# Top-k attention and a mixer block on one core: q and k transposed by the vector engine from 32 x 32 blocks, and one way of masking for all batches

## The chip, the cores and the metric

The kernel runs on one core of one Trainium2 chip. A core has five engines with queues of their own: TensorE (PE in the profile, with its weight loads as PEld), VectorE (DVE), ScalarE (ACT), GpSimd (POOL) and SyncE (SP), which here only issues transfers. All data are float32. The metric is the device time of one execution in microseconds (us), the median of several runs.

## The reference

Eight batches, eight heads, 576 positions, 64 features a head. Attention keeps, in each row of scores, those that are at least the 32nd largest; the rest get weight 0. The result, with the heads side by side (512 channels), goes through a mixer: a low-rank product along the sequence (rank 32) that is added to its input, and two dense layers of 2048 hidden channels with a ReLU.

```python
def _attn_ref(q, k, v):                       # (8, 8, 576, 64) each
    scores = 1 / sqrt(64) * np.matmul(q, k.transpose(0, 1, 3, 2))
    kth = np.partition(scores, -32, axis=-1)[..., -32:-31]
    scores = np.where(scores >= kth, scores, -1e9)
    attn = np.exp(scores - np.max(scores, axis=-1, keepdims=True))
    attn = attn / (np.sum(attn, axis=-1, keepdims=True) + 1e-9)
    return np.matmul(attn, v)

def _moe_ref(x, U, V, w_ch1, w_ch2):          # x: (8, 576, 512)
    h = x.transpose(0, 2, 1) @ U @ V
    u = x + h.transpose(0, 2, 1)
    return u + np.maximum(u @ w_ch1, 0.0) @ w_ch2
```

## The kernel before

The kernel works on pairs of heads, g = 0 to 31, four to a batch (NPAIR = 4). The 576 positions of a pair are five rows of tiles, t = 0 to 4: four of 128 positions, in which each head is a chunk of 128 x 576 scores, and a last one of 64 positions, in which both heads lie in one chunk (64 partitions each). So a pair has nine chunks. A step n of the main loop is one row: g, t = divmod(n, 5). The instructions of PE, ACT, DVE and POOL stand in the order in which the program makes them; the order of SyncE's transfers is left to a scheduler.

Loading and transposing. q and k come with positions on the partitions; TensorE transposes them, four tiles of 128 x 128 to a PSUM buffer, and ScalarE copies them to SBUF, so that features lie on partitions in qkT. Each pair has three such pieces: q, k, and the ends of both (the last 64 positions).

```python
    def load(g):
        b, h0 = g // NPAIR, 2 * (g % NPAIR)
        ends = loads.tile([P, 2, D], F32, tag="ld_ends", name="ld_ends")      # pool loads: bufs=1
        for name, src in (("q", q), ("k", k)):
            t = loads.tile([P, NT, 2, D], F32, tag=f"ld_{name}", name=f"ld_{name}")
            for i in range(2):
                # one transfer a head, on SyncE's queue (two of the first pair on ScalarE's)
                queue.dma_start(t[:, :, i, :], src[b, h0 + i, 0:MAIN, :].rearrange("(p t) d -> p t d", t=NT))
        # ... two transfers for the ends, five for v (into va, vd, vt, three buffers of each)

    def prep(g):
        # ...
        for i in (0, 2, 1) if g == 0 else (0, 1, 2):
            if i == 2:
                tp = ps_t.tile([P, 2, TAIL], F32, tag="tp", name="tp")        # ps_t: two PSUM buffers
                nc.tensor.transpose(tp.rearrange("p i n -> p (i n)"), ends.rearrange("p h d -> p (h d)"), ident)
                nc.scalar.copy(qkT[:, :, MAIN:S], tp)
                yield
                continue
            tp = ps_t.tile([P, NT, P], F32, tag="tp", name="tp")
            for c in range(NT):
                nc.tensor.transpose(tp[:, c, :], tiles[i][:, c].rearrange("p h d -> p (h d)"), ident)   # L272
            copy = nc.vector.tensor_copy if g == 0 and i else nc.scalar.copy
            copy(qkT[:, i, 0:MAIN], tp.rearrange("p t n -> p (t n)"))                                   # L274
            yield
```

The top 32 of a chunk. VectorE finds eight maxima at a time (L352, L366) and takes them out of a copy (L362), four and three times. The eighth of the last maxima is the row's threshold. After that there are three ways to the weights E, by chunk:

- early: ScalarE takes the exponential of all scores ahead, and VectorE then sets those below the threshold to 0 and sums the rest (L372).
- pooled: GpSimd compares and adds a huge negative number to the scores below the threshold (L369, L370), and ScalarE takes the exponential and the sum afterwards (L318).
- gaps: ScalarE makes relu((threshold - score) x 2^96) (L386, L387), GpSimd subtracts that (L388), and ScalarE takes the exponential and the sum (L318).

```python
    def ways(g, t):                               # chunks that are (early, pooled, gaps)
        if g < 2 * NPAIR and (g, t) != (NPAIR - 1, NT):
            if (g, t) == (NPAIR - 1, NT - 1):
                return (0,), (), (1,)
            return (), (1,) if t < NT else (), (0,)
        return (0,), (1,) if t < NT else (), ()

    def eased(g, t):
        return bool(ways(g, t)[2])

    def front(g, t):                              # a generator; the main loop takes it piece by piece
        # ... maxima and match_replace, four pieces
        for c in pooled:
            nc.gpsimd.tensor_scalar(Es[c], chunks[c], ms[c][:, 7:8], NEG, ALU.is_lt, ALU.mult)
            nc.gpsimd.tensor_tensor(chunks[c], chunks[c], Es[c], ALU.add)
        for c in early:
            nc.vector.scalar_tensor_tensor(out=Es[c], in0=chunks[c], scalar=ms[c][:, 7:8], in1=Es[c],
                                           op0=ALU.is_ge, op1=ALU.mult, accum_out=sums[c])
        # ...
        yield
        for c in gaps:
            least = small.tile([P, 1], F32, tag="least", name="least", bufs=3)
            nc.scalar.mul(least, ms[c][:, 7:8], WIDEN)
            nc.scalar.activation(Es[c], chunks[c], AF.Relu, bias=least, scale=-WIDEN)
            nc.gpsimd.tensor_tensor(chunks[c], chunks[c], Es[c], ALU.subtract)
            yield
        for c in order:
            if c not in early:
                weigh(chunks[c], Es[c], nmax[:, c : c + 1], sums[c])          # L318, the exponential
        # ...
```

After that TensorE transposes E (turns: L408 twice, four tiles each, then L413 once, with copies L409 and L414 on ScalarE), multiplies by v (values: L442, L445, and L432 for the last row), and after the fifth row of a pair turns the result and makes the low-rank product (mixed: L466, L477, L489, L491). Scores of the next row are L300 (L287 for the last row), copied to SBUF by ScalarE (L311 to L313, L294).

The mixer's dense layers of one batch (mlp: L514 and L533, 128 x 256 or 128 x 320 a matmul; L561 turns the result back) are laid between the steps of a later batch by `fill()`, so much a step, at 0.91 of the full share up to step 42. The main loop from the second batch on:

```python
        ease = eased(*divmod(n - 1, CH))          # here = front of row n, last = front of row n - 1
        # ... (the first batch and the turn to the second)
        if ease:
            next(last, None)
        fill()
        next(turning, None)
        fill()
        next(turning, None)
        if eased(*divmod(n - 2, CH)):
            next(turning, None)
        fill()
        next(ready, None)                         # ready = prep(g + 1), made at t == 1
        fill()
        if ease:
            next(last, None)
        if n - 2 >= ALONE:
            values(*divmod(n - 2, CH))
        if n + 1 < STEPS:
            scores(*divmod(n + 1, CH))
        next(here, None)
        next_params(1)
        # ...
        fill()
        next(here, None)
        fill()
        if n <= STEPS:
            turning = turns(*divmod(n - 1, CH))
        if not ease:
            next(turning, None)
        fill()
        next(here, None)
        next(last, None)
        # ...
        next(here, None)
        fill()
```

Of the kernel before, what the change touches and what calls it, by code (L numbers as in the profile page):

```python
# [8 lines left out]
F32 = mybir.dt.float32  # L9
# [17 lines left out]
def kernel(  # L27
# [28 lines left out]
    nc = tc.nc  # L56
    B, H, S, D = q.shape
    P = 128
# [4 lines left out]
    NT, TAIL = 4, 64  # L63
    MAIN = NT * P
    HALF = S // 2
    assert S == MAIN + TAIL and D == 64 and H % 2 == 0 and C == 512 and TOPK % 8 == 0
    NPAIR = H // 2
    NP = B * NPAIR
    SCALE = 1.0 / float(D) ** 0.5
    NV = 3  # L70
    HT = 10
    PE, ACT = mybir.EngineType.PE, mybir.EngineType.Activation
    DVE, POOL = mybir.EngineType.DVE, mybir.EngineType.Pool
# [2 lines left out]
    loads = ctx.enter_context(tc.tile_pool(name="loads", bufs=1))  # L76
# [18 lines left out]

    vas = [const.tile([P, 2, NT, D], F32, name=f"va{i}") for i in range(NV)]
    vds = [const.tile([P, P], F32, name=f"vd{i}") for i in range(NV)]
    vts = [const.tile([P, 2, D], F32, name=f"vt{i}") for i in range(NV)]

    xs = [const.tile([P, NT + 1, P], F32, name=f"x{i}") for i in range(2)]  # L100
    for i in range(NV):
        nc.gpsimd.memset(vds[i], 0.0)
# [25 lines left out]
    def half(h):  # L128
        return slice(h * D, (h + 1) * D)
# [97 lines left out]
    raw, qkTs, S2s, uTs, XTs, dens = {}, {}, {}, {}, {}, {}  # L227
    probs, PTs = {}, {}

    def load(g):  # L230
        b, h0 = g // NPAIR, 2 * (g % NPAIR)
        tiles = []
        ends = loads.tile([P, 2, D], F32, tag="ld_ends", name="ld_ends")
        for name, src in (("q", q), ("k", k)):
            t = loads.tile([P, NT, 2, D], F32, tag=f"ld_{name}", name=f"ld_{name}")
            for i in range(2):
                queue = nc.scalar if g == 0 and i else nc.sync
                queue.dma_start(
                    t[:, :, i, :],
                    src[b, h0 + i, 0:MAIN, :].rearrange("(p t) d -> p t d", t=NT),  # L240
                )
            tiles.append(t)
        for i, src in enumerate((q, k)):
            nc.sync.dma_start(
                ends[half(i)], src[b, h0 : h0 + 2, MAIN:S, :].rearrange("h p d -> p h d")
            )
        va, vd, vt = (a[g % NV] for a in (vas, vds, vts))
        for i in range(2):
            nc.sync.dma_start(
                va[:, i], v[b, h0 + i, 0:MAIN, :].rearrange("(p t) d -> p t d", t=NT)  # L250
            )
            nc.sync.dma_start(vd[half(i), half(i)], v[b, h0 + i, MAIN:S, :])
        nc.sync.dma_start(vt[TAIL:P], v[b, h0 : h0 + 2, MAIN:S, :].rearrange("h p d -> p h d"))
        raw[g] = tiles, ends

    def prep(g):

        tiles, ends = raw.pop(g)
        qkT = attn.tile([P, 2, S], F32, tag="qkT", name="qkT")
        qkTs[g] = qkT  # L260
        for i in (0, 2, 1) if g == 0 else (0, 1, 2):
            if i == 2:
                tp = ps_t.tile([P, 2, TAIL], F32, tag="tp", name="tp")
                nc.tensor.transpose(
                    tp.rearrange("p i n -> p (i n)"), ends.rearrange("p h d -> p (h d)"), ident
# [10 lines that stand above are left out]
# [44 lines left out]
    def ways(g, t):  # L320

        if g < 2 * NPAIR and (g, t) != (NPAIR - 1, NT):
            if (g, t) == (NPAIR - 1, NT - 1):
                return (0,), (), (1,)
            return (), (1,) if t < NT else (), (0,)
        return (0,), (1,) if t < NT else (), ()

    def eased(g, t):  # L330
        return bool(ways(g, t)[2])

    def front(g, t):
# [16 lines left out]
        for c in order:  # L350
            ms[c] = first[:, c]
            nc.vector.max(ms[c], curs[c])  # L352
        yield
        early, pooled, gaps = ways(g, t)
        for i in range(1, TOPK // 8):
            if i == 1:
# [60 lines left out]
    def inverse(g, lo, hi):  # L417
        den = dens[g][:, lo:hi]
        if g == NPAIR - 1:
            nc.vector.tensor_scalar_add(den, den, 1e-9)  # L420
        nc.vector.reciprocal(den, den)

    def values(g, t):

        PT = PTs.pop((g, t))
        va, vd, vt = (a[g % NV] for a in (vas, vds, vts))
        O = ps_t.tile([P, P], F32, tag="tp", name="O")
# [76 lines left out]
    def mlp(b):  # L504
# [3 lines left out]
        for chunks, (lo, hi) in zip(PARTS, SPAN):  # L508
            w = hi - lo
            hTs = []  # L510
            for f in range(NF):
# [11 lines left out]
                if f % 2 == 0:  # L523
                    hT = mlpp.tile([P, 2, WIDE], F32, tag="hT", name="hT", bufs=HT)
                    hTs += [hT[:, 0], hT[:, 1]]
# [53 lines left out]
    CH = NT + 1  # L579
# [30 lines left out]
    t = 0  # L610
    for _ in prep(0):
        pass
    scores(0, 0)
    turning = ready = iter(())
    fronts = {}
    for n in range(STEPS + 2):
        g, t = divmod(n, CH)
        if n < STEPS:
            if t == 0 and g + 1 < NP:
                load(g + 1)  # L620
            if t == 1 and g + 1 < NP:
                ready = prep(g + 1)
            fronts[n] = front(g, t)
            next(fronts[n])
        here, last = fronts.get(n, iter(())), fronts.pop(n - 1, iter(()))
        if n >= ALONE - 1 and n <= ALONE:

            if n < ALONE:
                next(last)
                values(*divmod(n - 3, CH))  # L630
                list(turning)
                next(here)
                next(last)
                scores(*divmod(n + 1, CH))
                values(*divmod(n - 2, CH))
            list(turns(*divmod(n - 1, CH)))
            values(*divmod(n - 1, CH))
            if n < ALONE:
                next(here)
                next(here)  # L640
                inverse(g, 0, 2 * NT)
                mixing.append(mixed(g, 1))
                fill()
                next(here)
# [3 lines that stand above are left out]
            next(here)  # L648
            while mixing:
# [4 lines that stand above are left out]
            next(here)  # L654
            fill()
            next(here)
            next(here)
            fill()
            continue
        ease = eased(*divmod(n - 1, CH))  # L660
        if n < ALONE:
# [3 lines that stand above are left out]
            if n >= 3:  # L665
                values(*divmod(n - 3, CH))
                if (n - 3) % CH == NT:
                    mixing.append(mixed((n - 3) // CH, 3))
            list(turning)
            fill()  # L670
            next(here)
            if t < NT:
                next_params(1)
            fill()
            next(ready, None)
            next(here)
            next(last, None)
            fill()
            next(here)
            if t in (0, 1):  # L680
                next_params(1)
            next(here)
            fill()
            if n >= 1:
# [5 lines that stand above are left out]
        next(turning, None)  # L690
        fill()
        next(turning, None)
        if eased(*divmod(n - 2, CH)):
            next(turning, None)
        fill()
        next(ready, None)
        fill()
        if ease:
            next(last, None)
# [6 lines that stand above are left out]
        if n - 2 >= ALONE and (n - 2) % CH == NT:  # L706
            mixing.append(mixed((n - 2) // CH, 5))
        fill()
        next(here, None)
        fill()  # L710
        if n <= STEPS:
            turning = turns(*divmod(n - 1, CH))
        if not ease:
            next(turning, None)
        fill()
        next(here, None)
        next(last, None)
        if t in (1, 3):
            next_params(1)
        next(here, None)  # L720
        fill()
# [33 lines left out]
```

## Time and profile before

| | before |
|---|---|
| time, median of 3 runs | 1842.92 us (1842.66 to 1843.83) |
| span of the profiled execution | 1841.4 us |
| mean granted TensorE clock | 0.974 |
| PE busy | 1739.0 us, 94% |
| PEld busy | 1319.0 us, 72% |
| DVE busy | 1561.2 us, 85% |
| ACT busy | 1020.7 us, 55% |
| POOL busy | 682.3 us, 37% |
| transfers | 58.20 MB in 127294 packets |

The profile is of one execution. A group of instructions is named by line of the kernel, engine, operation and tiles, output before input: "L272 PE MATMUL tp<-ident,ld_q" is a matmul of line 272 that writes tile tp from tiles ident and ld_q. "<-" after an idle time names what ended it. The chain of waits is followed back from the last instruction: at each step to what released it, or to the instruction ahead of it on its engine. In a timeline of engines the time of a matmul holds its latency, so that successive matmuls overlap; in the chain they are laid end to end. A line of one of the stretches of time gives the busy us of each engine in it.

### The profile page before, as it was taken

The page shows a single profiled execution, that of the slowest core. Times are in us where ns is not written, and L with a number is a line of the kernel's source. Part 1 is how long each engine was busy: PE and PEld are TensorE (multiplying, and loading weights), DVE is VectorE, ACT ScalarE, POOL GpSimd, SP SyncE. Part 2 cuts the span into 40 slices and gives each one's busy share as a digit, 9 for nine tenths or more (in the row PEclk, how much of TensorE's full clock was granted, in tenths as well). Part 3 has the DMA queues.
Part 4 walks back from the last instruction along what each step waited for, and adds up shares of the span by engine and source line. Part 5 has one row for each costly group of instructions (what it writes and reads, how often), then busy time and mean ns, then how long its engine had stood idle before and what let it go on. Part 6 is the DMA issues. An engine that isn't in the chain of part 4 may idle for free.

```text
span 1841.4 us, 29144 instructions
## 1 busy us (share of the span) xinstructions
PE 1739.0 (94%) x10528; PEld 1319.0 (72%) x10528; DVE 1561.2 (85%) x3208; ACT 1020.7 (55%) x2518; POOL 682.3 (37%) x471
## 2 busy tenths in 40 slices
PE   4666889999999999999999999999999999999999
PEld 2344566787777877788777877788777877778677
DVE  7999998999999999999999999999999999995000
ACT  4777777665545555555555555555555555454110
POOL 4777576543333323323233233323233333332000
PEclk7777999999999999999999999999999999999999
DMA  4232221101010000111010010110001010000000
GB/s 110 78 89 84 66 77 48 31 23 30 20 28 23 18 23 20 31 25 31 15 25 20 24 29 21 30 25 24 23 13 31 21 32 19 10 8 7 6 15 12
DMA packets 127294, 58.20 MB, mean 32 GB/s; under 512 B 89904, under 2 KB 124976, under 8 KB 127152
## 3 DMA queue, kind: packets, MB, share of 16 engines
q1 hardware_dynamic: 126096, 56.10, 11.6%
q8 instruction: 83, 1.36, 0.3%
q14 instruction: 59, 0.48, 0.1%
q10 hardware_dynamic: 1056, 0.26, 0.1%
HBM read 46.89 MB, written 9.44 MB: 31 GB/s over the span
## 4 chain that ended last, share of the span: by engine, by line
PE 82%; DVE 9%; ACT 5%; POOL 2%; issue 1%; DMA 0%; SPq 0%; POOLq 0%; ACTq 0%; DVEq 0%
PE mm L533 26%; PE mm L514 25%; PE sc L300 7%; PE O L445 6%; PE tp L408 6%; DVE rr L362 4%; DVE m L366 3%; PE sc L287 2%; PE O L432 2%; PE up L489 2%; PE O L442 1%; ACT E L318 1%; PE tp L272 1%; DVE first L352 1%; PE up L491 1%
## 5 line engine op out<-in xcount | busy, mean ns | idle before, releaser
L366 DVE MAX8 m<-rr 128x8 f32<-128x576 f32 x864 | 614.7, 748 | 5.5
L533 PE MATMUL mm<-hT,w 128*128 128x256 f32 (+1 forms) x2048 | 558.5, 410 | 0.0
L514 PE MATMUL mm<-uT,w 128*128 128x256 f32 (+1 forms) x2048 | 553.8, 411 | 1.1 <-ACT hT L526 1.1
L369 POOL TENSOR_SCALAR E<-Ssb,m 128x576 f32<-128x576 f32 x127 | 281.7, 2218 | 618.2 <-DVE m L366 550.0
L514 PEld LDWEIGHTS mm<-uT,w 128*128 128x128 f32 x2048 | 366.3, 191 | 106.8 <-issue 26.0
L533 PEld LDWEIGHTS mm<-hT,w 128*128 128x128 f32 x2048 | 363.3, 191 | 100.3 <-issue 22.5
L362 DVE MATCH_REPLACE8 rr<-m,rr 128x576 f32<-128x576 f32 x576 | 427.6, 742 | 0.0
L318 ACT ACTIVATE E<-Ssb,nmax 128x576 f32<-128x576 f32 x288 | 223.1, 776 | 25.0 <-POOL Ssb L370 15.6
L409 ACT COPY PT<-tp 128x512 f32<-128x512 f32 x288 | 167.9, 586 | 110.0 <-PE tp L408 108.0
L352 DVE MAX8 first<-Ssb 128x8 f32<-128x576 f32 x288 | 205.1, 749 | 21.8 <-ACT Ssb L313 21.7
L408 PE MATMUL tp<-ident,E 128*128 128x128 f32 x1152 | 179.3, 280 | 36.8 <-ACT XT L454 14.0
L362 DVE MATCH_REPLACE8 rr<-first,Ssb 128x576 f32<-128x576 f32 x288 | 211.8, 742 | 0.0
L408 PEld LDWEIGHTS tp<-ident,E 128*128 128x128 f32 x1152 | 142.3, 143 | 87.6 <-ACT E L318 20.1
L526 ACT ACTIVATE hT<-mm 128x320 f32<-128x320 f32 (+1 forms) x256 | 104.8, 409 | 142.7 <-PE mm L514 141.3
L370 POOL TENSOR_TENSOR Ssb<-Ssb,E 128x576 f32<-128x576 f32 x127 | 179.7, 1415 | 10.6
L300 PE MATMUL sc<-qkT 64*128 64x288 f32 x1024 | 169.3, 452 | 8.5 <-ACT Ssb L311 7.6
L372 DVE SCALAR_TENSOR_TENSOR E<-Ssb,m,E 128x576 f32<-128x576 f32 x122 | 100.8, 827 | 78.3 <-ACT E L318 67.5
L445 PE MATMUL O<-PT,va 128*64 128x128 f32 x2048 | 142.1, 282 | 0.0
L300 PEld LDWEIGHTS sc<-qkT 64*128 64x128 f32 x1024 | 92.7, 196 | 46.5 <-issue 16.6
L445 PEld LDWEIGHTS O<-PT,va 128*64 128x64 f32 x2048 | 111.0, 138 | 15.8 <-issue 0.9
L546 DVE TENSOR_TENSOR oT<-uT,mm 128x320 f32<-128x320 f32 (+1 forms) x8 | 3.6, 455 | 139.9 <-PE mm L533 139.9
L454 ACT COPY XT<-O 128x128 f32<-128x128 f32 x128 | 34.0, 266 | 135.8 <-PE O L445 135.8
(80 smaller groups left out, 1590.3 us busy)
## 6 DMA issues: line engine op xcount, KB each, us to landing
raw<-in_moe_w_ch_dram SPq DMA_DIRECT2D x32, 512.0 KB, 3.8
va<-in_v_dram SPq DMA_DIRECT2D x64, 128.0 KB, 2.4
out_dram<-ob SPq DMA_DIRECT2D x64, 128.0 KB, 1.9
ld_q<-in_q_dram SPq DMA_DIRECT2D x63, 128.0 KB, 2.8
ld_k<-in_k_dram SPq DMA_DIRECT2D x63, 128.0 KB, 2.7
ld_ends<-in_q_dram SPq DMA_DIRECT2D x32, 32.0 KB, 2.2
ld_ends<-in_k_dram SPq DMA_DIRECT2D x32, 32.0 KB, 2.2
vd<-in_v_dram SPq DMA_DIRECT2D x64, 16.0 KB, 2.0
```

Of the source, the lines that this page charges most:

```text
L300: nc.tensor.matmul(sc[:, h, 0:HALF], lhsT=qkT[half(h), 0, cols(t)], rhs=qkT[half(h), 1, i * HALF : (i + 1) * HALF], start=True, stop=True,)
L318: nc.scalar.activation(E, chunk, AF.Exp, bias=nmax, scale=SCALE, accum_out=total)
L352: nc.vector.max(ms[c], curs[c])
L362: nc.vector.match_replace(nxt, ms[c], curs[c], NEG)
L366: nc.vector.max(ms[c], curs[c])
L369: nc.gpsimd.tensor_scalar(Es[c], chunks[c], ms[c][:, 7:8], NEG, ALU.is_lt, ALU.mult)
L370: nc.gpsimd.tensor_tensor(chunks[c], chunks[c], Es[c], ALU.add)
L408: nc.tensor.transpose(tp[:, j, :], E2[:, a : a + P], ident)
L409: nc.scalar.copy(PT[:, NT * h : NT * h + NT], tp)
L445: nc.tensor.matmul(O[half(h)], lhsT=va[:, h, j, :], rhs=PT[:, NT * h + j], start=False, stop=(j == NT - 1),)
L514: nc.tensor.matmul(ph[:, 0:w], lhsT=w1[:, cc, f * P : (f + 1) * P], rhs=uT[:, cc, lo:hi], start=(cc == 0), stop=(cc == NC - 1),)
L533: nc.tensor.matmul(po[:, 0:w], lhsT=w2[:, f, c * P : (c + 1) * P], rhs=hTs[f][:, 0:w], start=(f == 0), stop=(f == NF - 1),)
```

## The change

From pair 5 on (the sixth), q and k are loaded in blocks of 32 positions by 32 features, each put where its transpose belongs, so that one VectorE instruction that transposes every 32 x 32 block (128 x 1152) makes qkT. It takes the place of nine TensorE transposes and three ScalarE copies. The first five pairs are loaded and transposed as before; all pairs share one load buffer now. To make room on VectorE, batches 2 to 7 are masked as batches 0 and 1 were: one chunk of a row by gap, the other by GpSimd, none by VectorE. The main loop is put in order for that: a row's three transposes of E stand each between fillers, and the vector transpose of the next pair stands at the end of the step.

```diff
     def load(g):
         b, h0 = g // NPAIR, 2 * (g % NPAIR)
-        tiles = []
-        ends = loads.tile([P, 2, D], F32, tag="ld_ends", name="ld_ends")
-        ...                                       # as shown above
+        ld = loads.tile([P, 2 * S], F32, tag="ld", name="ld")
+        if blocked(g):
+            for i, src in enumerate((q, k)):
+                for a in range(4):
+                    ds = src[b, h0 + a // 2, :, a % 2 * BLK : (a % 2 + 1) * BLK]
+                    to = ld[a * BLK : (a + 1) * BLK, i * S : (i + 1) * S]
+                    nc.sync.dma_start(
+                        to[:, 0:MAIN].rearrange("i (t m d) -> i t m d", t=NT, d=BLK),
+                        ds[0:MAIN].rearrange("(m i t) d -> i t m d", i=BLK, t=NT),
+                    )
+                    nc.sync.dma_start(
+                        to[:, MAIN:S].rearrange("i (m d) -> i m d", d=BLK),
+                        ds[MAIN:S].rearrange("(m i) d -> i m d", i=BLK),
+                    )
+            raw[g] = ld
+        else:
+            ...                                   # the former loads, into parts of ld
+    def blocked(g):
+        return g > NPAIR
     def prep(g):
-        tiles, ends = raw.pop(g)
         qkT = attn.tile([P, 2, S], F32, tag="qkT", name="qkT")
         qkTs[g] = qkT
+        if blocked(g):
+            nc.vector.transpose(qkT.rearrange("p i n -> p (i n)"), raw.pop(g))
+            yield
+            return
+        tiles, ends = raw.pop(g)
         ...
     def ways(g, t):
-        if g < 2 * NPAIR and (g, t) != (NPAIR - 1, NT):
-            if (g, t) == (NPAIR - 1, NT - 1):
-                return (0,), (), (1,)
-            return (), (1,) if t < NT else (), (0,)
-        return (0,), (1,) if t < NT else (), ()
+        if (g, t) == (NPAIR - 1, NT - 1):
+            return (0,), (), (1,)
+        if (g, t) == (NPAIR - 1, NT):
+            return (0,), (), ()
+        return (), (1,) if t < NT else (), (0,)
     ...                                           # main loop
         next(turning, None)
         fill()
         next(turning, None)
-        if eased(*divmod(n - 2, CH)):
-            next(turning, None)
-        fill()
-        next(ready, None)
+        fill()
+        next(turning, None)
         fill()
         if ease:
             next(last, None)
     ...
         fill()
         if n <= STEPS:
             turning = turns(*divmod(n - 1, CH))
-        if not ease:
-            next(turning, None)
         fill()
         next(here, None)
-        next(last, None)
+        next(ready, None)
         if t in (1, 3):
             next_params(1)
         next(here, None)
```

More of the change, by code (lines that the diff above doesn't have):

```diff
@@ L70 @@
     NV = 3
+    BLK = 32
     HT = 10
@@ L231, in load @@
         b, h0 = g // NPAIR, 2 * (g % NPAIR)
-        tiles = []
-        ends = loads.tile([P, 2, D], F32, tag="ld_ends", name="ld_ends")
[L234 to L240, printed above, removed]
-                )
-            tiles.append(t)
@@ L243, in load @@
[L243 to L246, printed above, removed]
+        ld = loads.tile([P, 2 * S], F32, tag="ld", name="ld")
[14 more added lines that the diff above has]
+        else:
+            tiles = []
+            ends = ld[:, 2 * MAIN : 2 * S].rearrange("p (h d) -> p h d", h=2)
+            for j, src in enumerate((q, k)):
+                t = ld[:, j * MAIN : (j + 1) * MAIN].rearrange("p (t h d) -> p t h d", t=NT, h=2)
+                for i in range(2):
+                    queue = nc.scalar if g == 0 and i else nc.sync
+                    queue.dma_start(
+                        t[:, :, i, :],
+                        src[b, h0 + i, 0:MAIN, :].rearrange("(p t) d -> p t d", t=NT),
+                    )
+                tiles.append(t)
+            for i, src in enumerate((q, k)):
+                nc.sync.dma_start(
+                    ends[half(i)], src[b, h0 : h0 + 2, MAIN:S, :].rearrange("h p d -> p h d")
+                )
+            raw[g] = tiles, ends
@@ L253, in load @@
         nc.sync.dma_start(vt[TAIL:P], v[b, h0 : h0 + 2, MAIN:S, :].rearrange("h p d -> p h d"))
-        raw[g] = tiles, ends
+    def blocked(g):
+        return g > NPAIR
     def prep(g):
-        tiles, ends = raw.pop(g)
         qkT = attn.tile([P, 2, S], F32, tag="qkT", name="qkT")
         qkTs[g] = qkT
+        if blocked(g):
[3 more added lines that the diff above has]
+        tiles, ends = raw.pop(g)
         for i in (0, 2, 1) if g == 0 else (0, 1, 2):
```

## The prediction

> **What bounds the kernel now.** I read the table by stretches of time first, because a share of the whole span mixes stages. Columns: stretch, PE, PEld, DVE, ACT, POOL busy us (and instructions), clock, DMA share, GB/s.
>
> ```profile
> 100.00:200.00 100.00, 60.74 (x405) 40.77 (x401) 98.73 (x202) 80.84 (x191) 76.53 (x53) 0.78 0.31 87
> 300.00:400.00 100.00, 97.75 (x625) 75.50 (x624) 86.78 (x177) 65.76 (x174) 54.03 (x37) 1.00 0.11 26
> 1000.00:1100.00 100.00, 99.80 (x636) 80.39 (x635) 94.19 (x196) 54.98 (x136) 33.89 (x22) 1.00 0.10 26
> 1700.00:1750.00 50.00, 48.68 (x201) 35.34 (x200) 0.00 (x0) 9.52 (x23) 1.76 (x2) 1.00 0.02 6
> ```
>
> VectorE is full in the first 200 us; from about 300 us on TensorE is; from 1690 us on only the last batch's mixer runs. [...] I looked at the chain of waits in one stretch of the long stage (start, us, what):
>
> ```profile
> 1008.09 0.44 PE tp L408 x4
> 1008.52 2.59 PE mm L514 x12
> 1011.11 0.11 PE tp L413
> 1011.22 1.30 PE mm L514 x6
> 1012.52 0.44 PE tp L272 x4
> 1012.96 0.87 PE mm L514 x4
> 1013.82 1.11 PE O L432 x10
> ```
>
> Each piece starts where the last one ends: TensorE works without a gap, and the instructions go in a fixed order. So here the time is the sum of TensorE's own steps, and four transposes of q (L272) cost 0.44 us of it, not 4 x 273 ns (their latency). A period of four pairs, from the starts of L394 (once per pair) at 955.17 and 1166.92 us, is 211.75 us, 52.9 us a pair.
>
> The other engines' costs come from the groups by line and form (busy us, mean ns, idle before):
>
> ```profile
> L372 DVE SCALAR_TENSOR_TENSOR E<-Ssb,m,E 128x576 f32<-128x576 f32 x122 | 100.8, 827 | 78.3 <-ACT E L318 67.5 <-DVE m L366 1.0
> L388 POOL TENSOR_TENSOR Ssb<-Ssb,E 128x576 f32<-128x576 f32 x39 | 55.5, 1423 | 21.3 <-ACT E L387 20.9
> L387 ACT ACTIVATE E<-Ssb,least 128x576 f32<-128x576 f32 x39 | 30.3, 776 | 1.3
> L386 ACT ACTIVATE least<-m 128x1 f32<-128x1 f32 x39 | 7.8, 201 | 22.7 <-DVE m L366 22.6
> L274 ACT COPY qkT<-tp 128x512 f32<-128x512 f32 x63 | 36.8, 584 | 47.4 <-PE tp L272 47.4
> ```
>
> L386 to L388 ran 39 times: batches 0 and 1 are already masked by gap (ScalarE, then GpSimd). L372 ran 122 times: batches 2 to 7 are masked by VectorE. The change makes the second kind into the first.
>
> [...] No duration exists in the trace; MAX8 over 576 columns recurs every 0.71 us (two in 1.41), [...] so I take 1.3 us.
>
> **The change, part by part.** Pair = two heads; 32 pairs; the new path is for pairs 5 to 31, 27 of them.
>
> TensorE loses eight L272 and one L264 transposes a pair: 0.44 + 0.44 + 0.11 = 0.99 us, start to start. Times 27 is 26.7 us. The work for pairs 8 to 31 lies where TensorE has no gap, so it counts in full: 23.8 us. Pairs 5, 6, 7 are prepared between about 220 and 350 us, where VectorE or ScalarE is sometimes last: I count half of 2.97, 1.5 us.
>
> VectorE loses L372 with its accumulator read in 120 rows or so. Its next MAX8 starts 0.74 us after L372 did, so a pair's five rows give back 3.7 us. It gains 1.3 us for the transpose. Rows of top-k stay: about 5.04 us per chunk of 576 (a row of two chunks: 1009.71 to 1019.91, 10.2 us, with a 0.12 us reciprocal in it), nine chunks a pair, 45.4 us. Sum after: 45.4 + 0.1 + 1.3 = 46.8 us in a pair of 52, 90%; before 49.2 of 52.9, 93%. That is off the path: it frees time on an engine that is not the bound.
>
> ScalarE gains 5 x (0.20 + 0.78) for the gap and 5 x 0.19 for the sums, 5.9 us, and loses 0.58 + 0.58 + 0.27 = 1.4 us of qkT copies: from 55% to about 65%. GpSimd gains 5 x 1.42 = 7.1 us, from 34% to about 48%. Neither is full. The stretch 300 to 400 us is already like this, with parameter work besides (66% and 54%), and TensorE is at 97.75.
>
> The order of TensorE's pieces moves too: the third transpose of a row comes after one more filler. In the eased batches of before the second and third came together and the next piece waited for a PSUM buffer:
>
> ```profile
> 338.27 0.45 PE tp L408 x4
> ...
> 338.74 0.59 ACT PT L409
> ...
> 339.38 0.81 PE up L489 x2
> ```
>
> 339.38 - 338.72 = 0.66 us lost, and the same at 389.60 and 411.42 us: three in 85 us. Over the 170 us from 250 to 420 some 4 us; I count 2, as other waits remain.
>
> Loads: a pair's q and k were 2304 pieces of 256 bytes in 6 DMAs, and become 4608 of 128 bytes in 16. Two ld_q issues took 1.25 us, so 16 take 10 us of SyncE's queue and v's five another 3 us, in 52. The buffer is freed by the transpose of one pair and needed a pair later, some 50 us; a load lands in 2.8 us. It is hidden. At 27 ns a piece (11.6% of 16 x 1841.4 us over 126096 pieces) the added 62208 pieces are 1.7 ms over 16 engines, 6% of their span, where 10% is used.
>
> What it costs: the way from a row's last maximum to its weights gets longer. GpSimd then takes 2.2 + 1.4 + 1.4 = 5.1 us, the two exponentials about 2 us. A row of two chunks takes VectorE 10.1 us and scores are made about every 10 us, one row ahead, so a row's weights have 20 us from its scores and need 1.8 + 10.1 + 7.1 = 19. If they are late, ScalarE waits in order, and the copies behind them. TensorE has two mixer buffers in hand, some 2 us. So it fits, barely; I count 3 us of new gaps over the run.
>
> Sum: 1842.9 - 23.8 - 1.5 - 2 + 3 = 1818.6, say 1819 us, 1.3% less.
>
> **The rivals.** (a) VectorE's freed time is worth something: if L372 were on the path, 120 x 0.74 = 89 us less 35 us of transposes, 54 us gained, 1789 us. Against it: no VectorE in the chain from 420 to 1690 us; its 67.5 us of waits for L318 are idle time of an engine with room. (b) The gap's chain becomes the bound. For it: in the eased stage before, ScalarE waits for GpSimd:
>
> ```profile
> ACT E L318 <- POOL Ssb L370: 3.8, 2, 3.0
> DVE first L352 <- ACT Ssb L313: 15.0, 5, 5.8
> ```
>
> (waits from 300 to 420 us: total, times, longest). If 1 to 2 us a pair reached TensorE, the 27 us are eaten: 1820 to 1845 us; 4 us a pair would make 1890. Against it: there the starts of L394 are 53.1, 52.1 and 50.1 us apart (266.22 to 421.52), with 0.91 of the filler work. The mixer's two lines are 58% of the chain of the long stage, 30.9 us of a pair, so 9% is 2.8 us and TensorE's sum would be 50.1: 3, 2 and 0 us are lost, falling as the parameter work ends, and part of it is the PSUM wait that goes. (c) The transposes wait for 128-byte loads: each us of wait per pair that VectorE cannot absorb costs 27; 5 us of it stay hidden. Against it: the 50 us of lead. [...]
>
> **Range and chances.** The whole of TensorE's 26.7 us and 4 us of order give 1812; more than that has no source in the chain, so the low end is 1806, a little below. The high end, 1834, is (b) with 0.6 us a pair lost. Faster by over 2% needs under 1806 us and so rival (a): 0.08. Slower by over 2% needs (b) or (c) at over 2 us a pair: 0.06. Within 2%: 0.86.
>
> **What would show it.** Right: in the long stage a pair takes 51.9 to 52.3 us (from the line that takes L394's place), TensorE's transposes of q and k are left for the first five pairs only, VectorE at about 90% from 500 to 1600 us, its transpose near 1.3 us with no wait for a DMA. Wrong: ScalarE's wait for GpSimd in the chain of the long stage (b), VectorE waiting for the load (c), or a pair far under 51.9 us (a).

## The result and the profile after

The changed kernel takes 1817.49 us (median of 4 runs, 1816.63 to 1819.71) where the one before takes 1843.02: a ratio of 0.9863, with a 95% interval of 0.9846 to 0.9880. That is 1.4% less; 1819 us was predicted.

The stretches of time of the changed kernel, with the columns as in the prediction (stretch; PE, PEld, DVE, ACT, POOL busy us; clock; DMA share; GB/s):

```profile
100.00:200.00 100.00, 59.68 (x401) 40.27 (x396) 98.72 (x202) 79.84 (x189) 75.76 (x52) 0.78 0.29 83
...
300.00:400.00 100.00, 97.79 (x608) 74.64 (x604) 92.18 (x185) 65.55 (x173) 53.75 (x36) 1.00 0.13 26
...
1000.00:1100.00 100.00, 99.88 (x632) 78.19 (x631) 88.18 (x174) 62.58 (x164) 44.31 (x30) 1.00 0.12 25
```

The long stage looks as it did: TensorE is full, VectorE has fallen from 94 to 88, ScalarE and GpSimd have taken on the masks. The chain of waits in one stretch (start, us, what) shows the transposes of E, the mixer and the rest end to end, and none of q and k:

```profile
1007.58 0.44 PE tp L436 x4
1008.01 0.55 PE pT L505 x10
1008.57 1.06 PE mm L542 x4
1009.63 0.44 PE tp L436 x4
1010.06 0.54 PE up L517 x2
1010.61 0.39 PE up L519 x4
1010.99 0.92 PE mm L542 x4
1011.91 0.11 PE tp L441
1012.02 0.43 PE up L517 x2
```

L436 to L437, L441, L517 and L542 are the old L408, L409, L413, L489 and L514. At 1009.63 to 1012.02 the second and third transposes of a row stand apart, and the piece that needs a PSUM buffer no longer waits for a copy. The groups of instructions that are new or changed in number (count, then busy us, mean ns of one, idle before):

```profile
L416 POOL TENSOR_TENSOR Ssb<-Ssb,E 128x576 f32<-128x576 f32 x159 | 224.7, 1413 | 192.2 <-ACT E L415 190.8
...
L285 DVE STREAM_TRANSPOSE qkT<-ld 128x1152 f32<-128x1152 f32 x27 | 36.7, 1361 | 0.0
...
L302 ACT COPY qkT<-tp 128x512 f32<-128x512 f32 x9 | 5.2, 575 | 1.9 <-PE tp L300 1.9
...
L400 DVE SCALAR_TENSOR_TENSOR E<-Ssb,m,E 128x576 f32<-128x576 f32 x2 | 1.6, 792 | 0.1
```

The vector transpose takes 1.36 us and has no idle time before it, so no load is late. VectorE's masks are gone (2 of 122 left). From the waits, with total us, times and the longest:

```profile
DVE first L380 <- ACT Ssb L341: 129.0, 52, 5.4
...
ACT E L346 <- POOL Ssb L398: 22.6, 12, 3.7
```

VectorE now waits for the next row's scores, 129 us in all: it has time left over. ScalarE waits for GpSimd's masks for 22.6 us in the whole run, and none of that stands in the chain of the long stage.

To see where the time went I use one mark a pair, which stands at the same place of TensorE's order in every kernel: the start of L432 (the product with v of a pair's last row; L460 after). Two of them from each timeline, before and then after:

```profile
484.24 1.05 PE L432 MATMUL O<-va,PT 128*128 128x128 f32 x8
...
1648.45 1.05 PE L432 MATMUL O<-va,PT 128*128 128x128 f32 x8
```

```profile
480.80 1.05 PE L460 MATMUL O<-va,PT 128*128 128x128 f32 x8
...
1623.54 1.05 PE L460 MATMUL O<-va,PT 128*128 128x128 f32 x8
```

They are the marks of pairs 8 and 30, 22 pairs apart: 1164.21 us before and 1142.74 after, 52.92 and 51.94 us a pair. L394, from which the prediction took its period, would not do for a comparison: the change moves it within a step. The same marks of all kernels, from their timelines (us; one profiled execution of each, so the early column also holds what happened to the clock in that execution):

| kernel | up to mark of pair 7 | pair 8 | pairs 9 to 30, each | from there to the end |
|---|---|---|---|---|
| before | 431.48 | 52.76 | 52.92 | 192.95 |
| after | 427.38 | 53.42 | 51.94 | 192.96 |
| e1_transpose_only | 431.43 | 51.58 | 51.95 | 192.75 |
| e2_masks_only | 431.44 | 53.17 | 53.72 | 193.86 |
| e3_masks_and_order | 427.99 | 52.83 | 52.93 | 193.07 |
| e4_transpose_and_order | 427.10 | 53.46 | 51.94 | 192.99 |
| e5_double_transpose | 431.83 | 53.42 | 51.94 | 193.01 |
| e6_double_without_masks | 440.21 | 53.81 | 52.97 | 192.76 |
| e7_loads_of_256_bytes | 427.18 | 53.41 | 51.94 | 193.07 |
| e8_outputs_too | 426.45 | 49.49 | 51.38 | 189.32 |
| e9_double_new_order | 430.81 | 53.46 | 52.86 | 194.42 |
| e10_outputs_without_masks | 428.30 | 49.49 | 51.83 | 191.02 |

Of the 24.9 us between the two spans, 21.5 come from pairs 9 to 30, 4.1 from the time before, and pair 8 gives 0.7 back.

### The profile page after: what moved, and what is told of

It reads as the page before. It is cut to its first block, busy times and chain, and to the rows that moved or that the text cites. A ratio compares the mean times of both kernels' runs of the same rounds, so it can differ in the third digit from the quotient of the medians.

```text
span 1816.5 us, 28753 instructions
## 1 busy us (share of the span) xinstructions
PE 1715.5 (94%) x10285; PEld 1293.7 (71%) x10285; DVE 1498.8 (83%) x2995; ACT 1084.2 (60%) x2797; POOL 846.8 (47%) x591
## 2 busy tenths in 40 slices
DMA packets 193823, 58.21 MB, mean 32 GB/s; under 512 B 156432, under 2 KB 191504, under 8 KB 193680
## 3 DMA queue, kind: packets, MB, share of 16 engines
q1 hardware_dynamic: 192624, 56.11, 13.4%
## 4 chain that ended last, share of the span: by engine, by line
PE 81%; DVE 14%; POOL 2%; ACT 1%; issue 1%; DMA 0%; SPq 0%; POOLq 0%; DVEq 0%; ACTq 0%
PE mm L542 26%; PE mm L561 26%; PE sc L328 7%; DVE rr L390 6%; PE O L473 6%; PE tp L436 6%; DVE m L394 5%; DVE first L380 2%; PE sc L315 2%; PE O L460 2%; PE O L470 2%; PE up L517 1%; PE tp L589 1%; PE up L519 1%; PE tp L494 1%
## 5 line engine op out<-in xcount | busy, mean ns | idle before, releaser
L394 DVE MAX8 m<-rr 128x8 f32<-128x576 f32 x864 | 614.9, 749 | 5.5
L542 PE MATMUL mm<-uT,w 128*128 128x256 f32 (+1 forms) x2048 | 546.1, 410 | 0.8 <-ACT hT L554 0.8
L542 PEld LDWEIGHTS mm<-uT,w 128*128 128x128 f32 x2048 | 368.3, 190 | 110.7 <-issue 25.6
L416 POOL TENSOR_TENSOR Ssb<-Ssb,E 128x576 f32<-128x576 f32 x159 | 224.7, 1413 | 192.2 <-ACT E L415 190.8
L437 ACT COPY PT<-tp 128x512 f32<-128x512 f32 x288 | 167.6, 586 | 125.3 <-PE tp L436 123.6
L346 ACT ACTIVATE E<-Ssb,nmax 128x576 f32<-128x576 f32 x288 | 221.0, 771 | 29.6 <-POOL Ssb L398 22.6
L436 PE MATMUL tp<-ident,E 128*128 128x128 f32 x1152 | 177.7, 279 | 37.9 <-ACT XT L482 15.3
L436 PEld LDWEIGHTS tp<-ident,E 128*128 128x128 f32 x1152 | 143.5, 143 | 86.2 <-ACT XT L482 17.1
L398 POOL TENSOR_TENSOR Ssb<-Ssb,E 128x576 f32<-128x576 f32 x127 | 178.9, 1409 | 10.6
L473 PE MATMUL O<-PT,va 128*64 128x128 f32 x2048 | 143.7, 284 | 0.0
L415 ACT ACTIVATE E<-Ssb,least 128x576 f32<-128x576 f32 x159 | 123.3, 776 | 5.2
L473 PEld LDWEIGHTS O<-PT,va 128*64 128x64 f32 x2048 | 112.3, 139 | 16.0 <-issue 1.1
```

Source lines behind the costliest of these rows:

```text
L346: nc.scalar.activation(E, chunk, AF.Exp, bias=nmax, scale=SCALE, accum_out=total)
L436: nc.tensor.transpose(tp[:, j, :], E2[:, a : a + P], ident)
L473: nc.tensor.matmul(O[half(h)], lhsT=va[:, h, j, :], rhs=PT[:, NT * h + j], start=False, stop=(j == NT - 1),)
L542: nc.tensor.matmul(ph[:, 0:w], lhsT=w1[:, cc, f * P : (f + 1) * P], rhs=uT[:, cc, lo:hi], start=(cc == 0), stop=(cc == NC - 1),)
```

## The experiments

Theory S: in the long stage the time is the sum of TensorE's own steps, and only what leaves that sum counts. Rival V: VectorE's freed time was worth something itself. Rival G: the longer way over GpSimd costs. Rival C: the small pieces of the loads cost. The change has three parts (transposes, masks, order of the loop); the first four kernels take them apart.

**e1_transpose_only**: the kernel before, with the loads and the vector transpose of the change.

```diff
+        if blocked(g):                            # load: blocks of 32 x 32, as in the change
+            nc.vector.transpose(qkT.rearrange("p i n -> p (i n)"), raw.pop(g))
     # ways() and the main loop as before
```

> Only the blocked loads and the vector transpose; masks and order of the loop as before, so VectorE keeps the 120 masking instructions of batches 2 to 7. Theory S (the time is TensorE's own sum in the long stage): VectorE would be at 49.2 + 1.36 = 50.6 of 51.95 us a pair, 97%, still under TensorE, and nearly the whole 0.99 us a pair comes: 1817 to 1824 us. Rival V (the masks had to leave VectorE for the gain to come): VectorE's full row of 10.9 us is longer than the step of about 10 us, delays are not made up, and the time stays at 1828 to 1843 us.

Measured: 1819.05 us, ratio to before 0.9869 (0.9854 to 0.9884). Nearly the whole gain, with the masks left on VectorE. Its long stage, 500 to 1600 us (columns as above):

```profile
500.00:1600.00 1100.00, 1098.68 (x6768) 837.89 (x6766) 1064.60 (x2163) 586.24 (x1455) 364.18 (x235) 1.00 0.12 24
```

VectorE is busy for 1064.60 of 1100 us, 96.8%, and TensorE still sets the pace. It waits for another engine for 11.7 us of them (L399 for L345's exponentials). Theory S holds here and rival V does not. Up to the mark of pair 7, though, it gains nothing (431.43 against 431.48 us); the point on pairs 5 to 7 below says where that went.

**e2_masks_only**: the kernel before, with the masks of the change.

```diff
-        if g < 2 * NPAIR and (g, t) != (NPAIR - 1, NT):
-            ...
-        return (0,), (1,) if t < NT else (), ()
+        ...
+        return (), (1,) if t < NT else (), (0,)
     # loads and the main loop as before
```

> Only the masks: all batches by gap and GpSimd, loads and order of the loop as before. It takes 89 us of masking from VectorE. Theory S: no gain from that; and the second and third transposes of a row now come together, with a PSUM wait of 0.66 us each time that the next piece needs a buffer; three were seen in 85 us, so some 44 in the 1270 us of the long stage, 29 us: 1855 to 1875 us. Rival V (VectorE's time is on the path): 1790 to 1830 us. Rival G (the longer way over GpSimd costs): over 1880 us, with ScalarE waiting for GpSimd in the chain.

Measured: 1861.82 us, ratio 1.0100 (1.0083 to 1.0117). Taking the masks from VectorE without the new order makes the kernel slower. The chain of waits shows why:

```profile
1030.39 1.06 PE mm L514 x4
1031.45 0.45 PE tp L408 x4
1031.90 0.02 issue
1031.92 0.59 ACT PT L409
1032.52 0.04 issue
1032.56 0.81 PE up L489 x2
```

The second and third transposes come together, and L489 waits 0.66 us for a PSUM buffer. TensorE's waits from 485 to 1665 us (total, times, longest) hold nothing else:

```profile
PE up L489 <- ACT PT L409: 12.5, 22, 0.6
```

That is 22 waits, one a pair. At 0.66 us each they make 14.5 of the 17.5 us that pairs 9 to 30 lose; the other 3 us stay open. I had reckoned with 44: three in one stretch of 85 us were too few to count from. The direction was right, the size was half. Rivals V and G fall: the time is far above the one range and below the other.

**e3_masks_and_order**: masks and order of the change, with TensorE's transposes of q and k.

```diff
     # load() and prep() as before; ways() and the main loop of the change
```

> The masks and the new order of the loop, with the old loads and TensorE's transposes of q and k. It differs from the changed kernel by the transposes alone. Theory S: it lies 25 to 27 us above the changed kernel's 1817.5, at 1841 to 1845 us, a pair 52.9 us. Rival V: under 1830 us. If the order and the masks gave part of the gain by themselves: 1832 to 1840 us.

Measured: 1840.55 us, ratio 0.9983 (0.9977 to 0.9990). It lies 23 us above the changed kernel, and its pairs take 52.93 us, as before. So the freed VectorE gives nothing in the long stage. It gains 3.5 us up to the mark of pair 7, though, where the prediction had counted 2 us for the order and the range of theory S none, and so lies half a us under that range.

**e4_transpose_and_order**: the changed kernel with batches 2 to 7 masked by VectorE again; the last piece of such a row is taken at the end of the step, as before.

```diff
     # ways() as before; load(), prep() and the main loop of the change, and in it:
+        if not ease:
+            next(last, None)
         next(ready, None)
```

> Blocked loads, vector transpose and the new order, but batches 2 to 7 masked by VectorE as before. Theory S: as e1_transpose_only within 3 us, and so 1815 to 1824 us: TensorE has no gap that the order could fill in these batches. Rival V: 1828 to 1843 us, like e1_transpose_only. If e1_transpose_only is slow and this one is not, it is the order and not the masks that the transpose needed.

Measured: 1818.13 us, ratio 0.9865 (0.9850 to 0.9879), within 1 us of the changed kernel and of e1. The masks, by themselves, are worth less than can be told here. What e1 lacks before the mark of pair 7, this kernel has (427.10 us). Since e2 has nothing of it (431.44 us) and e3 has most of it without the transposes (427.99 us), that gain is mainly of the order.

The other six ask how much room VectorE had, whether the loads cost, and whether the idea carries further.

**e5_double_transpose**: each vector transpose of the changed kernel done twice.

```diff
-            nc.vector.transpose(qkT.rearrange("p i n -> p (i n)"), raw.pop(g))
+            for _ in range(2):
+                nc.vector.transpose(qkT.rearrange("p i n -> p (i n)"), raw[g])
```

> The changed kernel with each vector transpose done twice: 27 x 1.36 = 37 us more of VectorE's work, from about 89% to 92% in the long stage. Theory S: it is hidden, 1815 to 1821 us. Rival V: up to 37 us more, 1830 to 1855 us.

Measured: 1821.86 us, ratio 0.9881 (0.9866 to 0.9896), 4.4 us above the changed kernel and just over the range of theory S. All of it lies before the mark of pair 7 (431.83 against 427.38); from pair 9 on a pair takes 51.94 us, to the hundredth. The long stage hides it wholly; the early stage does not, and I had not allowed for that. It is not simply 1.36 us a pair: 3.8 us are lost by the mark of pair 4 (277.96 against 274.14), ahead of which one doubled transpose stands (226.72 us). TensorE there waits 4.6 us for one result of ScalarE, in a chain over GpSimd's and ScalarE's work on the parameters without VectorE, and the granted clock is then 0.57 from 240 to 244 us. How the doubling leads to that is open.

**e6_double_without_masks**: e1_transpose_only, with each vector transpose done twice (the edit of e5).

> As e1_transpose_only (masks and order as before, 1819.05 us), with each vector transpose done twice. VectorE was at 96.8% there and comes to 99.4% of a pair. It asks how near VectorE was to being the bound. Theory S in its strict form (only the larger sum counts): 1817 to 1823 us. If VectorE needs room for its waits, it sets the pace: up to 37 us more, 1826 to 1856 us; then the masks bought the room.

Measured: 1849.71 us, ratio 1.0033 (1.0019 to 1.0048). Here 27 x 1.36 = 37 us of VectorE's work cost 31 us. The strict form of theory S, that only the larger of the two sums counts, falls. But there was a second cause to suspect: in the old order the transposes stand ahead of a reciprocal on VectorE, and ScalarE waits for that one (61.6 us in 15 times from 500 to 1600 us).

**e9_double_new_order** takes that away: e4_transpose_and_order, with each vector transpose done twice.

> As e6_double_without_masks (two vector transposes a pair, masks by VectorE, 1849.71 us), but in the new order of the loop, where the transposes stand at the end of a step and no longer between a row's first maxima and the reciprocal that ScalarE waits for. If the loss of e6 came from VectorE being full (99.4% of a pair), it stays: 1840 to 1852 us. If it came from where the transposes stood: 1818 to 1828 us.

Measured: 1843.75 us, ratio 1.0004 (0.9995 to 1.0012), 25.6 us above e4. Most of the loss stays, so it is not where the transposes stood. The long stage, and a stretch of its chain of waits:

```profile
500.00:1600.00 1100.00, 1084.63 (x6637) 820.08 (x6636) 1076.68 (x2138) 576.73 (x1432) 355.99 (x228) 1.00 0.12 24
```

```profile
1011.64 0.83 DVE E L402 x2
1012.47 1.33 DVE first L382 x2
1013.80 0.06 DVE den L451
1013.86 1.45 DVE rr L392 x2
1015.32 1.32 DVE m L396 x2
1016.63 0.74 DVE rr L392
```

In this stretch the chain is VectorE's from end to end; over the whole stage it is VectorE's for about two fifths and TensorE's for most of the rest. What shows that VectorE is full is its list of waits, which is empty from 500 to 1600 us: the profile shows no wait of it for another engine, and yet its busy time is 1076.68 of 1100 us, 97.9%. The rest, 23.3 us, is short gaps between its 2138 instructions, 11 ns each on average. So e1, at 96.8%, had about one per cent of room, the 11.7 us of its waits. In e9 a pair takes 52.86 us on average, and one more transpose is in it than in e4; less 1.36 that is 51.5 us of VectorE's own against TensorE's 51.94.

**e7_loads_of_256_bytes**: the changed kernel, with pairs 5 to 31 loaded as before in pieces of 256 bytes. The blocks are then not transposed to where they belong, and scores are made of other numbers.

```diff
-        if blocked(g):                            # load
+        if False:
     ...
-            raw[g] = tiles, ends
+            raw[g] = ld if blocked(g) else (tiles, ends)
```

> The changed kernel, but pairs 5 to 31 load q and k as before (6 transfers in pieces of 256 bytes instead of 16 in pieces of 128) and the vector transpose is kept; blocks are then not where they belong, so the scores are of other numbers and the output is not the reference's. It leaves the work of all engines as it is. Theory S: loads are hidden, 1815 to 1820 us. Rival C (the small pieces cost): over 3 us faster, under 1814 us.

Measured: 1818.20 us, ratio 0.9865 (0.9848 to 0.9881). The changed kernel has 193823 packets and this one 127293, and the DMA share of the long stage is 0.12 and 0.09; nothing of it reaches the time. Rival C falls.

**e8_outputs_too**: the changed kernel, and the mixer's result is also turned back by the vector transpose and stored from its blocks. TensorE loses 160 transposes and ScalarE their copies. The vector transposes stand a step later than the result, so that VectorE does not wait for it in the long stage (it waits three times in the whole run, 27.8 us); the result has four buffers for that.

```diff
-            for i, t in enumerate(chunks):
-                nc.tensor.transpose(tp[0:n, i, :], oT[:, OFF[t] - lo : OFF[t] - lo + n], ident)
-            ...                                   # two copies on ScalarE, one or two stores
+            nc.vector.transpose(ob[:, 0:w], oT[:, 0:w])
+            for a in range(4):                    # stores of 32 x 32 blocks, two or three for each a
+                queue.dma_start(out[b, 0:MAIN, cs].rearrange("(m i t) d -> i t m d", i=BLK, t=NT)[:, t + i], ...)
```

> The same idea carried on: the result of the mixer is turned back by the vector transpose (64 of 320 or 256 columns) and stored in pieces of 128 bytes, instead of 160 TensorE transposes and their copies on ScalarE. Theory S: 160 x 0.109 = 17.4 us off TensorE's sum, 1798 to 1803 us; VectorE gains some 23 us, which is hidden. If VectorE waits for the result of the mixer in its order, or the small stores hold up buffers: 1806 to 1825 us.

Measured: 1798.38 us, ratio 0.9754 (0.9739 to 0.9768): 19 us under the changed kernel, and faster than both. A pair takes 51.38 us, 0.56 less; a pair's five transposes at 0.109 us are 0.55. Pair 8 gains 3.9 us besides (TensorE has no wait there for the result of the mixer any more, and the granted clock stays at 1.00), and the time after the last mark 3.6 us.

**e10_outputs_without_masks**: the same with batches 2 to 7 masked by VectorE (the edit of e4).

> As e8_outputs_too (1798.38 us), but batches 2 to 7 masked by VectorE as before. By sums VectorE has 50.3 + 2 x 0.46 = 51.2 of a pair of 51.4 us, 99.7%. Theory S in its strict form: 1797 to 1803 us. If VectorE needs room, as e6 showed: 1810 to 1835 us, and the masks, worth about 1 us in the change itself, are what lets the next step pay.

Measured: 1809.68 us, ratio 0.9817 (0.9801 to 0.9833), just under the range that I had given for a VectorE without room. A pair takes 51.83 us instead of 51.38. Here the masks are worth 11 us. VectorE is as full as in e9, with one wait of 0.5 us in the long stage:

```profile
500.00:1600.00 1100.00, 1092.55 (x6680) 827.52 (x6680) 1076.85 (x2205) 568.33 (x1394) 362.35 (x235) 1.00 0.13 23
```

Less its two transposes of outputs, on average 0.49 and 0.42 us in e8, a pair here leaves 50.9 us for the rest of VectorE's work, where e9 gave 51.5: VectorE's own sum in the change without its masks is known to about half a us.

## Why the prediction was right, point by point

**TensorE's sum in the long stage** (23.8 us from pairs 8 to 31 at 0.99). Right. Pairs 9 to 30 gained 21.5 us, 0.98 each, and e1, e3 and e4 show that it is the transposes that gave it: with them a pair takes 51.94 or 51.95 us whatever the masks and the order are, without them 52.92 or 52.93. In e1, which has the old order, the way from the mark of pair 6 to that of pair 7, which holds most of the work for pair 8, is 1.00 us shorter than before (50.33 against 51.33), and pair 8 is 1.18 us shorter; with 21.4 us in pairs 9 to 30 that is 23.6 of the 23.8 us.

**Half of the gain for pairs 5 to 7** (1.5 us). Wrong in size. e1 is 1.19 us ahead at the mark of pair 5 (328.22 against 329.41) and 0.95 us behind at that of pair 6 (381.10 against 380.15). In between TensorE waits 1.24 and 0.57 us for ScalarE's copies, and the chain leads from there back over ScalarE and then, almost without a gap, through VectorE's work to its transpose at 326.84 us: here VectorE has no room. After these waits the clock falls:

```profile
340.00:342.00 2.00, 2.00 (x8) 1.63 (x7) 1.97 (x6) 0.43 (x1) 1.33 (x1) 0.57 0.60 165
342.00:344.00 2.00, 2.00 (x7) 1.44 (x7) 2.00 (x5) 0.24 (x1) 0.00 (x0) 0.58 0.12 25
```

At 0.57 and 0.58 for 4 us some 1.7 us are lost, by estimate (2 us x 0.43 and 2 us x 0.42). The prediction had no term for that. In the new order, without this fall, the transposes give 0.6 us (the changed kernel against e3) to 0.9 (e4 against e3) up to the mark of pair 7.

**The order** (2 us). Too small: 3.5 us up to the mark of pair 7 (e3). The 4.3 us between e4 and e1 hold e1's fall of the clock. Part of it is given back in pair 8, below. The two terms of the early stage were off in opposite directions, about 0.9 too much and 1.5 too little, and so their sum, 3.5 us against 4.1 measured, came out near by luck.

**New gaps** (3 us over the run). They were expected spread out, from masks that are late. In the long stage there are none: e3 with its masks on GpSimd takes 52.93 us a pair, before 52.92. Some 1.8 us were lost in one place, pair 8 (53.42 us against 51.58 in e1), and it is not the masks, as e4 has it too (53.46). The chain of the changed kernel there:

```profile
438.49 0.74 POOL oT L577
439.22 0.04 issue
439.27 0.45 PE tp L589 x2
439.72 0.02 issue
439.74 0.38 ACT ob L591
440.12 0.04 issue
440.17 0.72 PE up L517 x2
...
441.74 1.91 PE O L473 x16
```

TensorE waits for the mixer's last result, then for a PSUM buffer, and the next pieces run slowly: L473 takes 1.91 us instead of 1.02. The stretches of time give the clock:

```profile
440.00:442.00 2.00, 1.83 (x10) 1.51 (x12) 1.97 (x6) 0.93 (x4) 0.00 (x0) 0.68 0.36 89
442.00:444.00 2.00, 2.00 (x18) 1.67 (x16) 1.70 (x3) 1.51 (x5) 0.79 (x1) 0.50 0.26 38
```

A granted clock of 0.68 and 0.50 for 4 us. The kernels e4, e5, e7 and e9, which have both waits too, show the same fall, to between 0.50 and 0.54; e6 has one wait of 1.9 us there, and falls to 0.51. Why it comes is open: e3 has waits of the same length (1.25 and 0.45 us) and e2 of 1.3 and 0.6 us, and their clock stays at 1.00; before and e1 have the first wait alone, and no fall there.

**VectorE**: 90% of a pair was predicted, 981 of 1100 us, 89%, was measured, and the transpose took 1.36 us (27 of them, 1.358 to 1.366) where 1.3 was my estimate, from no run: the kernel before has no such instruction. The rate of MAX8 that stands beside it does not give 1.3 us, and it came from a misread line: two MAX8 in 1.41 us are first start to last end, and laid end to end in a chain two take 1.32 (e9), so one recurs every 0.66 us and not every 0.71. GpSimd came to 46% (48 predicted), ScalarE to 61% (65). I had added mean durations, but instructions of an engine overlap and their busy time counts that once: ScalarE's groups from 500 to 1600 us add up to 768.5 us, and its busy time is 674.70. GpSimd started lower than I had read from one stretch of 100 us, at 354 of 1100 us, 32% and not 34%.

**Loads**: right, hidden (e7). The pieces were priced too high: 6 points of the DMA engines' time were reckoned, and the queue's share went from 11.6% to 13.4%.

**The rivals**: none came. The figures of (b) do not follow from its terms: 1 to 2 us a pair over the 24 pairs of the long stage are 24 to 48 us, which gives 1843 to 1867 us and not 1820 to 1845, and 4 us a pair would give 1915, not 1890.

**What the prediction left out**: it called VectorE's freed time worthless. For this change it nearly is (e4: under 1 us). But it took the sums alone for the test, and e9 and e10 show that VectorE is full at about 98% busy, so that the change without its masks stood 0.4 to 1 us a pair from a new bound. The masks are room for the next step: with the outputs transposed as well they are worth 11 us (e8 against e10).

## What to carry to other kernels

When one engine works without a gap in a fixed order, price a change by the start-to-start time of what leaves that engine, and take work off it to whichever engine has time left; then ask what the second engine's busy share becomes, for it can be the bound a few per cent below 100, as VectorE here at 97.9; its list of waits tells. A transfer that has to happen anyway can place blocks so that a block-wise transpose is a whole one, in loads and in stores. Compare kernels at a mark that stands at the same place in the bound engine's order, and count rare waits over the whole stage, not over a short stretch.

## What the runs showed of the hardware that I had not expected

VectorE, without a wait for another engine in 1100 us, showed 97.9% busy (e9); in the full stretch from 100 to 200 us it showed 98.7%. TensorE's granted clock fell to between 0.50 and 0.58 for some 4 us after short waits in the midst of full stages: after two waits of together 1.7 us in five kernels at pair 8, after one of 1.9 us in e6, after two of together 1.8 us in e1 at 340 us. It did not after two waits of together 1.7 us in e3 and 1.9 us in e2, so the length of the waits alone does not decide. The change makes 66,500 packets more, and that cost no time that can be measured (1817.49 us with them, 1818.20 without, e7).
